# Reordering the start of two MoE layers: table behind the gathers, splits behind the activations, transposes on TensorE

## The chip, the cores and the metric

The kernel runs on one core of a Trainium2 chip. The metric is device time in microseconds of one execution, the median of the runs. The engines are TensorE (PE in the profile, its weight loads PEld), VectorE (DVE), ScalarE (ACT), GpSimd (POOL) and SyncE (SP), which here only issues DMAs; each runs its own instructions in order and waits on semaphores for the others.

## What is computed

Sparse attention over 4 batches, 8 heads, 576 positions and head size 64 (four heads with a window of 32, four with every fourth of 128 positions), then two mixture-of-experts layers with one expert for each of 2304 tokens.

```python
def reference(...):
    attn = softmax(where(mask, q @ k.T / 8, -1e9)) @ v      # 4 x 8 x 576 x 64
    x = attn.transpose(0, 2, 1, 3).reshape(2304, 512)
    # first MoE, 8 experts, w1 512 x 1024, w2 1024 x 512
    e = argmax(x @ w_gate)
    x = softmax(x @ w_gate)[e] * sigmoid(x @ w_output_gate)[e] * (relu(x @ w1[e]) @ w2[e])
    # second MoE, same shapes
    l = x @ w_gate2 + modality_bias[modality_id]
    e = argmax(l)
    return softmax(l)[e] * (relu(x @ w1b[e]) @ w2b[e])
```

Every float32 factor of a product is held as a high and a low float16 part ("hi" and "lo"), and three of the four products are summed. So each expert's weights, 4 MB in float32, are loaded to `raw`, and split: the high part on ScalarE (L100), the low part on VectorE (L105) or GpSimd.

## The kernel before

**The attention** runs over 16 head pairs in an order written out by hand (`ORDER`, `iteration`), and ends in `tail` (L556), where the last two pairs are finished while the weights of the first expert are split: `his` splits high parts on ScalarE, `los` low parts on VectorE. A piece is 1024 columns of `raw`; there are eight, four of w1 and four of w2. Before the tail, in iteration 14, `lo_in_place` (L111) makes the low part of piece 0 with two GpSimd instructions (L113, L114). `stM` (L394) builds the softmax mask of a pair from six tiny operations, on VectorE for the last pair; `stMT` transposes it on TensorE and copies it on ScalarE (L425). `stH` (L467) and `stZ` (L474) split a pair's result; `stZ` runs on GpSimd except for the last pair. `fs()` steps `first_slots`, which finds the first 256 tokens of the commonest expert and gathers their rows.

**Each MoE** (`moe`, L885) works through slots of 128 tokens. `slot` (L956) multiplies with w1 in two halves of 48 products (`mm1`), applies relu and splits each half (`hsplit`: high on ScalarE L943, low on VectorE L944), and multiplies with w2 in 24 products (L1006): for each of eight chunks the high part with w2's high and low part, then the low part with w2's high part. Slots 0, 1 and 2 use the first expert; slot 3 (`KE`) is the first with weights that the sorted table chooses. Around a slot's products lie numbered hooks; `at(s, k, ...)` puts work at hook k of slot s, in the order in which the engines get it. Hook 1 lies inside the first half of the w1 products, hook 2 after it, 3 after the first `hsplit`, 5 after the second, 9 and 6 after 4 and 12 of the 24 products, 7 after the last.

**The sort** (`sort`, L708) is a generator whose steps are placed at hooks. It computes each token's expert and rank; `ob` and `obp` (one-hot of the block, L811, L812); `table()` (L776), some twenty VectorE operations that decide which expert each slot has; the rank matrix `A` (L820); with `A` and `obp` on TensorE the index of each slot's tokens (L825); gathers of three slots' rows on GpSimd (L896); then the gates, and at the end two sums over `A` (L871, L873). In the first MoE `first` is true: `obp` is made on GpSimd, and `table()` with the eight weight loads of slot 3 (`start.weights`) comes ahead of `A`. In the second MoE they come after the gathers.

`first_splits(FIRST[i])` splits two pieces of slot 3's weights and loads the two after them for slot 4. `x_turned` (L907) brings the gathered rows of a slot into column form by eight TensorE transposes and a ScalarE copy; `x_transpose` (L899) does it by a DMA transpose. `post1.out` (L1132) scales a slot's result and splits it into a row; `post1.transposes` (L1143) stores the row and, for results 0 and 1 (`TURN` is 2), turns it by a DMA transpose; `post1.turn` (L1152) turns later ones on TensorE; `post1.router` multiplies with the second router's weights.

## Time and profile before

| what | us |
|---|---|
| median of 3 runs | 660.13 (657.55 to 660.41) |
| profiled execution, its own time | 657.82 |
| its span, first to last instruction | 656.0 |
| TensorE busy | 595.0 (91% of the span) |
| VectorE busy | 364.8 (56%) |
| ScalarE busy | 271.0 (41%) |
| GpSimd busy | 206.6 (31%) |
| mean granted clock of TensorE | 0.967 |

The attention takes the first 155 us, the first MoE runs to about 436 us, the second from there. In the profile an idle stretch of an engine is put down to the instruction that released it ("PE plg L1168 <- DMA yT" says that TensorE waited at line 1168 for the DMA that wrote `yT`). The granted clock is a share of 2.4 GHz; 0.50 is 1.2 GHz. Times in a timeline are microseconds from the span's start: start, duration, engine, line, operation, output and inputs, count.

### The profile page before, as it was taken

The numbers are of one execution on the slowest core, as the hardware profiler recorded it, in microseconds if no ns is written. First come the engines' busy times: TensorE is split into PE (matmuls) and PEld (weight loads), VectorE is DVE, ScalarE is ACT, GpSimd is POOL, SyncE is SP. The second block draws the span as 40 slices with busy tenths as digits, with TensorE's granted clock in tenths as the row PEclk, the third lists the DMA queues.
The fourth block names the chain that finished last, engine by engine and source line by source line (L and its number), as shares of the span: only waits on it lengthen the run. The fifth ranks groups of instructions, "written<-read, shape, count | busy, mean of one in ns | idle before, by whom it ended". The sixth has DMA issues, their size and how long they took to land. (4 is left out here: it accounts for less than half of the span.)

```text
span 656.0 us, 19386 instructions
## 1 busy us (share of the span) xinstructions
PE 595.0 (91%) x7393; PEld 461.0 (70%) x7393; DVE 364.8 (56%) x638; ACT 271.0 (41%) x368; POOL 206.6 (31%) x319
## 2 busy tenths in 40 slices
PE   3989798867888999999999999989899999999994
PEld 2878787756656776868677686766576768677772
DVE  6798888888576625963848922249531011113560
ACT  5667676763165124833626611111522112113450
POOL 3657676823282111101010410002542312122220
PEclk9989989986898999999999999999989999999998
DMA  8764849952599973997876862210995424132921
GB/s 281 247 204 160 237 165 314 263 128 69 193 308 263 267 163 86 332 358 159 204 220 203 222 143 67 57 30 23 309 304 124 117 64 98 50 98 84 310 59 40
DMA packets 105088, 115.20 MB, mean 176 GB/s; under 512 B 68623, under 2 KB 73487, under 8 KB 104976
## 3 DMA queue, kind: packets, MB, share of 16 engines
q1 hardware_dynamic: 99296, 95.94, 52.2%
q0 software_dynamic: 5280, 17.13, 8.2%
q8 instruction: 59, 0.97, 0.6%
q10 hardware_dynamic: 400, 0.72, 0.3%
q14 instruction: 53, 0.43, 0.2%
HBM read 209.13 MB, written 18.22 MB: 347 GB/s over the span
## 5 line engine op out<-in xcount | busy, mean ns | idle before, releaser
L933 PEld LDWEIGHTS <-wb 128*128 128x128 f16 x4032 | 233.5, 99 | 10.2 <-DMA xT<-xg 2.6
L933 PE MATMUL ph<-xT,wb 128*128 128x128 f16 x3648 | 214.3, 221 | 3.9 <-DMA xT<-xg 2.6
L944 DVE SCALAR_TENSOR_TENSOR hl<-ph,hh 128x512 f16<-128x512 f32 x84 | 57.7, 689 | 171.5 <-ACTq L952 156.8
L1006 PE MATMUL py<-wb,hh 128*128 128x512 f16 x608 | 137.9, 379 | 0.7 <-ACT hh L943 0.6
L1006 PEld LDWEIGHTS <-hh 128*128 128x128 f16 x672 | 63.6, 98 | 71.6 <-ACT hh L943 3.7
L943 ACT ACTIVATE hh<-ph 128x512 f16<-128x512 f32 x84 | 50.1, 596 | 154.2 <-PE ph L933 147.8
L105 DVE SCALAR_TENSOR_TENSOR wb<-raw,wb 128x1024 f16<-128x1024 f32 (+1 forms) x79 | 103.6, 1350 | 16.2 <-ACT wb L100 13.8
L100 ACT ACTIVATE wb<-raw 128x1024 f16<-128x1024 f32 (+1 forms) x80 | 87.0, 1134 | 7.7 <-ACTq L952 3.0
L1006 PE MATMUL py<-wb,hl 128*128 128x512 f16 x304 | 71.8, 379 | 0.0
L1006 PEld LDWEIGHTS <-hl 128*128 128x128 f16 x336 | 32.9, 98 | 39.6
L1268 POOL DMA_INDIRECT out<-y,idx x16 | 16.1, 1009 | 100.9 <-ACTq L952 84.0
L452 PE MATMUL po<-v,pT 128*96 128x65 f32 x384 | 41.1, 260 | 0.0
L452 PEld LDWEIGHTS po<-v,pT 128*96 128x96 f32 x384 | 38.0, 176 | 0.0
L391 PE MATMUL ps<-kk,qs 128*96 128x128 f16 x192 | 31.1, 235 | 4.1 <-DVE kk L349 2.2
L391 PE MATMUL ps<-kk,ql 128*96 128x128 f16 x192 | 31.3, 236 | 3.5 <-DVE ql L369 3.4
L439 ACT ACTIVATE pT<-pst 128x384 f32<-128x384 f32 x48 | 23.5, 489 | 24.6 <-PE pst L438 23.9
L896 POOL DMA_INDIRECT xg<-x_dram,idxaa x23 | 25.1, 1090 | 26.5 <-DMA xT<-xg 14.3
L392 DVE TENSOR_REDUCE M<-ps 96x4 f32<-96x512 f32 x48 | 31.6, 680 | 3.2 <-PE ps L391 2.8
L391 PEld LDWEIGHTS <-ql 128*96 128x96 f16 x192 | 24.7, 135 | 12.4 <-DVE ql L369 5.1
L436 PE MATMUL pst<-mt,msel 128*128 128x96 bf16 x192 | 30.9, 220 | 2.1 <-ACT mt L425 2.1
L1267 ACT ACTIVATE y<-py,gsb 128x512 f32<-128x512 f32 x16 | 11.0, 686 | 52.4 <-PE py L1006 49.5
L391 PEld LDWEIGHTS <-qs 128*96 128x96 f16 x192 | 25.0, 135 | 8.6 <-issue 4.1
(404 smaller groups left out, 739.0 us busy)
## 6 DMA issues: line engine op xcount, KB each, us to landing
raw<-in_w1a SPq DMA_DIRECT2D x95, 512.0 KB
raw<-in_w2a SPq DMA_DIRECT2D x92, 512.0 KB
raw<-in_w1b SPq DMA_DIRECT2D x75, 512.0 KB
raw<-in_w2b SPq DMA_DIRECT2D x72, 512.0 KB
qk<-in_qk SPq DMA_DIRECT2D x16, 608.0 KB
v<-in_vw SPq DMA_DIRECT2D x16, 390.0 KB
y_dram<-y SPq DMA_DIRECT2D x11, 260.0 KB
y_dram<-lotmp SPq DMA_DIRECT2D x10, 260.0 KB
```

The lines of the kernel that those rows point to most:

```text
L100: nc.scalar.activation(wb[:, 0, s], raw[:, s], AF.Copy, scale=SW)
L105: nc.vector.scalar_tensor_tensor(out=wb[:, 1, s], in0=raw[:, s], scalar=SW, in1=wb[:, 0, s], op0=ALU.mult, op1=ALU.subtract)
L391: nc.tensor.matmul(ps[:, j, :], q[:, h, QT * i:QT * i + QT], kk[:, h, QT * i:QT * i + 128], start=False, stop=w == 1 and j == 3, skip_grou ...
L392: nc.vector.tensor_reduce(out=Ms[n][:, 4 * g:4 * g + 4], in_=ps, axis=AX.X, op=ALU.max)
L436: nc.tensor.matmul(ps[:, j, :], msel[:, typ, j, :], mt[:, g, :], start=j == 0, stop=False, skip_group_check=True)
L439: nc.scalar.activation(pTs[n][:, 4 * g:4 * g + 4, :], ps, AF.Exp, scale=0.125 / (SQK * SQK))
L452: nc.tensor.matmul(po[:, h, i, :], pT[:, NQ * h + i, :], v[:, h, i, :], start=True, stop=True)
L896: nc.gpsimd.indirect_dma_start(t, None, src, bass.IndirectOffsetOnAxis(start.idx[:, s:s + 1], 0))
L933: nc.tensor.matmul(ph[:, j, :], w[:, c, fs], xT[:, parts[c + i], :], start=k == 0, stop=k == 47, skip_group_check=True)
L943: nc.scalar.activation(hs, ph, AF.Relu)
L944: nc.vector.scalar_tensor_tensor(out=hl[:, 4 * g:4 * g + 4, :], in0=ph, scalar=0.0, in1=hs, op0=ALU.max, op1=ALU.subtract)
L1006: nc.tensor.matmul(to, a, w, start=k == 0, stop=k == len(ops) - 1)
```

## The change

- `TURN` becomes 0: no result is turned by a DMA transpose. Results 0 and 1 are turned by TensorE after slot 2 of the first MoE (hook 7), result 1 through the PSUM buffer `pw`, and written out at hooks 5 and 6, behind both activations.
- `lo_in_place` goes; the low parts in `tail` are each one piece earlier, and those of pieces 6 and 7 are made in slot 0. `stZ` runs on VectorE for the last two pairs.
- In the first MoE's sort `obp` is made on VectorE, and `table()` with slot 3's loads comes after the index and the gathers, as in the second MoE. The index is computed within slot 0's second products, at a new hook 10 behind the 20th.
- In slot 0 of the first MoE the second products are in the order high x high, low x high, high x low.
- The splits of slot 3's weights move behind the activations: in the first MoE from hooks (1,3), (1,6), (2,0), (2,1) to (1,5), (1,6), (2,0), (2,3); in the second the first of them from (2,3) to (2,5).
- The rows of slot 3 are turned by TensorE in slot 2 of both MoEs, at hook 1 of the first and hook 2 of the second, instead of by a DMA transpose issued in slot 1.

```diff
@@ -30,7 +30,7 @@
 CA1, CA2, CF = 13, 13, 4
 KA, KE = 2, 3
 NMIN = 18
-TURN = KE - 1
+TURN = 0
 NB = 12
 BIG = 8e12
 SQK = 2.0 ** 5
@@ -107,11 +107,6 @@
         else:
             nc.gpsimd.tensor_scalar(pool[:, 0:n * 512], raw[:, s], SW, None, op0=ALU.mult)
             nc.gpsimd.tensor_tensor(wb[:, 1, s], pool[:, 0:n * 512], wb[:, 0, s], op=ALU.subtract)
-
-    def lo_in_place(wb, k, n=2):
-        s = slice(k * 512, (k + n) * 512)
-        nc.gpsimd.tensor_scalar(raw[:, s], raw[:, s], SW, None, op0=ALU.mult)
-        nc.gpsimd.tensor_tensor(wb[:, 1, s], raw[:, s], wb[:, 0, s], op=ALU.subtract)
 
     def splits(wb, ops, load=None):
 
@@ -471,7 +466,7 @@
             kind = hp // 2
             x16, xh = x16s[b, kind], x_half[b, kind]
             c = slice((hp % 2) * 128, (hp % 2) * 128 + 128)
-            (nc.vector if n == NPR - 1 else nc.gpsimd).tensor_tensor(x16[:, :, 1, c], xh[:, :, c], x16[:, :, 0, c], op=ALU.subtract)
+            (nc.vector if n >= NPR - 2 else nc.gpsimd).tensor_tensor(x16[:, :, 1, c], xh[:, :, c], x16[:, :, 0, c], op=ALU.subtract)
             if hp % 2 == 0:
                 return
 
@@ -556,12 +551,12 @@
         def tail():
             a, b = NPR - 2, NPR - 1
             his(2, 3)
-            los(1)
+            los(0)
             stC(a, 0)
             stH(b - 2)
             stMT(b)
             his(4)
-            los(2, 3)
+            los(1, 2)
             stZ(b - 2)
             stB(b, 0)
             stC(a, 1)
@@ -576,7 +571,7 @@
             his(7)
             stB(b, 2)
             stZ(a)
-            los(4)
+            los(3)
             stC(b, 0)
             fs()
             stX(a, 0)
@@ -589,11 +584,11 @@
             stR(a - 2)
             stR(b - 2)
             stZ(b)
-            los(5)
+            los(4)
             stX(b, 0)
             stX(b, 1)
             stR(a)
-            los(6)
+            los(5)
             fs()
             stR(b)
 
@@ -643,8 +638,6 @@
                     do(f, n + dn, *x)
                 if n == NPR - 2 and o in ('H', 'MT'):
                     his(o == 'MT')
-                if n == NPR - 2 and o == 'P1':
-                    lo_in_place(wbuf[0], 0)
 
         STEP = {'A': (stA, 1), 'B': (stB, 0), 'C': (stC, -1), 'X': (stX, -2), 'K': (khi, 2), 'L': (klo, 2), 'Q': (qsc, 2), 'P': (qsplit, 2)}
         STEP = {k + str(i): v + (i,) for k, v in STEP.items() for i in range(3)}
@@ -705,7 +698,7 @@
             return t
         return T
 
-    def sort(nm, lg, nt, inv, fe, ea, tab, scale, og, extra, gscale, start, first):
+    def sort(nm, lg, nt, inv, fe, ea, tab, scale, og, extra, gscale, start):
 
 
         v, gp, act = nc.vector, nc.gpsimd, nc.scalar
@@ -809,11 +802,8 @@
         sb = [P, nt, NSLOT]
         ob, obp = (T(k, [-1, NSLOT], F16) for k in ("ob", "obp"))
         v.tensor_tensor(ob, bm.unsqueeze(1).to_broadcast(sb), pi[:, 1].unsqueeze(2).to_broadcast(sb), op=ALU.is_equal)
-        (gp if first else v).tensor_tensor(obp, ob, tokv[:, :nt].unsqueeze(2).to_broadcast(sb), op=ALU.mult)
-        yield
-        if first:
-            table()
-            start.weights(KE, always=True)
+        v.tensor_tensor(obp, ob, tokv[:, :nt].unsqueeze(2).to_broadcast(sb), op=ALU.mult)
+        yield
         A = T("A", [-1, P], F16)
         for a in range(0, nt, ACH):
             n = min(ACH, nt - a)
@@ -831,9 +821,8 @@
         start.idx, start.idxf = idx, idxf
         for i in range(KA, KA + 3):
             start.gather(i)
-        if not first:
-            table()
-            start.weights(KE, always=True)
+        table()
+        start.weights(KE, always=True)
         yield
 
         dl = T("dl", [-1, E])
@@ -1001,7 +990,8 @@
             sp(2)
             k = 0
             to = pys[s] if s < KA else py
-            ops = [(a[:, f, :], w[:, f, :]) for a, b_ in ((hh, (w2h, w2l)), (hl, (w2h,))) for f in range(8) for w in b_]
+            order = [(hh, (w2h,)), (hl, (w2h,)), (hh, (w2l,))] if start.late_low and s == 0 else [(hh, (w2h, w2l)), (hl, (w2h,))]
+            ops = [(a[:, f, :], w[:, f, :]) for a, b_ in order for f in range(8) for w in b_]
             for a, w in ops:
                 nc.tensor.matmul(to, a, w, start=k == 0, stop=k == len(ops) - 1)
                 k += 1
@@ -1009,6 +999,8 @@
                     hook(9)
                 if k == 12:
                     hook(6)
+                if k == 20:
+                    hook(10)
             if s >= NMIN - 1:
                 post.router(s - 1)
             elif s >= KE:
@@ -1038,7 +1030,7 @@
         return r
 
     class Start:
-        name, next = "a", NEXT
+        name, next, late_low = "a", NEXT, True
 
         def hook(self, s, k):
             for f in self.plan.get((s, k), ()):
@@ -1149,12 +1141,12 @@
                 return
             self.turn(s)
 
-        def turn(self, s):
+        def turn(self, s, tag="pyt"):
 
             if s is not None and s < TURN:
                 return
             y16 = self.row(s)
-            pt = pp.tile([P, 8, P], F16, name="pyt", tag="pyt")
+            pt = pp.tile([P, 8, P], F16, name=tag, tag=tag)
             for c in range(8):
                 nc.tensor.transpose(pt[:, c, :], y16[:, c * P:(c + 1) * P], identh)
             vt.tensor_copy(self.yT[0 if s is None else s % 2], pt)
@@ -1177,7 +1169,7 @@
                 vt.scalar_tensor_tensor(out=lg2[:, s, :], in0=pl, scalar=1.0 / (SX2 * SWR), in1=lg2[:, s, :], op0=ALU.mult, op1=ALU.add)
 
     post1 = Post1()
-    so1 = sort("a", lg1[:, :, 0:8], NT, None, fe1, early[0], tabs[0], 1 / (SX1 * SWR1), lg1[:, :, 8:16], [midf], SX2 / (SX1 * SW * SW), start1, True)
+    so1 = sort("a", lg1[:, :, 0:8], NT, None, fe1, early[0], tabs[0], 1 / (SX1 * SWR1), lg1[:, :, 8:16], [midf], SX2 / (SX1 * SW * SW), start1)
     fs2 = []
 
     def slots2():
@@ -1197,22 +1189,23 @@
     def at(s, k, *f):
         plan.setdefault((s, k), []).extend(f)
 
-    at(0, 0, run(so1), lambda: lo_piece(wbuf[0], 14))
+    at(0, 0, run(so1), lambda: lo_piece(wbuf[0], 12))
     at(0, 1, run(so1, 2))
     at(0, 2, run(fss))
-    at(0, 5, run(so1))
-    at(1, 0, run(so1, 2))
-    at(1, 3, run(so1), start1.consts, lambda: start1.first_splits(FIRST[0]))
-    at(1, 6, lambda: start1.turned(KA), lambda: start1.transpose(KA + 1), lambda: start1.first_splits(FIRST[1]))
-    at(2, 0, lambda: gt.memset(y16p[1][:, 2 * DM:], 0.0))
-    at(2, 0, lambda: start1.first_splits(FIRST[2]))
-    at(2, 1, lambda: start1.first_splits(FIRST[3]))
+    at(0, 5, run(so1), lambda: lo_piece(wbuf[0], 14))
+    at(0, 10, run(so1, 2))
+    at(1, 3, run(so1), start1.consts)
+    at(1, 5, lambda: start1.first_splits(FIRST[0]))
+    at(1, 6, lambda: start1.turned(KA), lambda: start1.first_splits(FIRST[1]))
+    at(2, 0, lambda: gt.memset(y16p[1][:, 2 * DM:], 0.0), lambda: start1.first_splits(FIRST[2]))
+    at(2, 1, lambda: start1.turned(KA + 1))
     at(2, 2, run(so1))
+    at(2, 3, lambda: start1.first_splits(FIRST[3]))
     for i in range(NSLOT - NMIN):
         at(0, 3, lambda i=i: start1.zero(i))
-    at(2, 3, first_out(post1, start1, 0))
-    at(2, 5, first_out(post1, start1, 1))
-    at(2, 6, lambda: start1.part(KE + 1, *EARLY))
+    at(2, 5, first_out(post1, start1, 0))
+    at(2, 6, first_out(post1, start1, 1))
+    at(2, 7, lambda: post1.turn(0), lambda: post1.turn(1, "pw"), lambda: start1.part(KE + 1, *EARLY))
     at(3, 7, start1.last)
     for s, k in ((3, 5), (3, 7), (4, 3), (4, 5), (4, 7), (5, 5)):
         at(s, k, run(fes2))
@@ -1229,7 +1222,7 @@
     ilast = m1.tile([P, 1], I32, name="ilast")
 
     class Start2(Start):
-        name, next = "b", NEXT2
+        name, next, late_low = "b", NEXT2, False
 
         def fields(self, g, inv, ex):
             self.g = g
@@ -1275,17 +1268,17 @@
             pass
 
     start2, post2 = Start2(), Post2()
-    so2 = sort("b", lg2, NSLOT, start1.inv, fe2, early[1], tabs[1], 1.0, None, [], 1 / (SX2 * SW * SW), start2, False)
+    so2 = sort("b", lg2, NSLOT, start1.inv, fe2, early[1], tabs[1], 1.0, None, [], 1 / (SX2 * SW * SW), start2)
     plan = start2.plan = {}
     at(0, 0, lambda: post1.out(None, py1), lambda: post1.transposes(None))
     at(0, 8, lambda: post1.router(None), run(so2))
     at(0, 5, run(so2))
     at(0, 7, run(so2, 2))
     at(1, 9, run(so2, 2))
-    at(1, 7, lambda: start2.turned(KA), lambda: start2.transpose(KA + 1))
+    at(1, 7, lambda: start2.turned(KA))
+    at(2, 2, lambda: start2.turned(KA + 1))
     at(2, 0, run(so2))
-    at(2, 3, lambda: start2.first_splits(FIRST[0]))
-    at(2, 5, lambda: start2.first_splits(FIRST[1]))
+    at(2, 5, lambda: start2.first_splits(FIRST[0]), lambda: start2.first_splits(FIRST[1]))
     at(2, 6, run(so2), lambda: start2.first_splits(FIRST[2]))
     at(2, 7, lambda: start2.first_splits(FIRST[3]))
     for i in range(KA):
```

`late_low` is true in the first MoE and false in the second.

## Rows read from the trace of the kernel before

**Rows 1.** Waits of TensorE, whole span (waiter, releaser: us in total, times, longest)

```profile
PE pm L423 <- DVE mb L413: 4.1, 1, 4.1
...
PE pidx L825 <- DVE Aa L820: 3.1, 2, 2.2
...
PE ph L933 <- DMA xT<-xg: 2.6, 1, 2.6
...
PE plg L1168 <- DMA yT<-y: 2.4, 1, 2.4
...
PE pya L1006 <- ACT hh L943: 1.5, 1, 1.5
...
PE pg L873 <- POOL lotmp L1207: 1.1, 1, 1.1
```

**Rows 2.** Windows: length, busy PE PEld DVE ACT POOL, clock, DMA share, GB/s

```profile
155.51:216.11 60.60, 51.84 (x586) 39.40 (x586) 42.75 (x90) 24.20 (x31) 24.65 (x41) 0.92 0.74 228
476.23:488.33 12.10, 12.10 (x121) 9.23 (x120) 4.32 (x6) 2.34 (x4) 5.91 (x10) 0.87 0.86 301
488.33:498.87 10.54, 10.54 (x122) 7.71 (x120) 1.38 (x2) 2.57 (x4) 2.56 (x4) 1.00 0.72 183
146.00:148.00 2.00, 1.86 (x36) 1.80 (x35) 1.35 (x4) 0.68 (x1) 0.00 (x0) 0.50 0.00 0
```

**Rows 3.** The timeline of the tail: start, us, engine, line, operation

```profile
129.64 2.12 POOL L114 TENSOR_TENSOR wb<-raw,wb 128x1024 f16<-128x1024 f32 x1
...
129.89 1.91 DVE L410 TENSOR_TENSOR r<-r,mb 96x12 f32<-96x12 f32 x1
...
131.14 0.82 ACT L467 CAST x<-xh 96x768 f16<-96x768 f32 x1
...
133.72 0.16 DVE L413 CAST mb<-r 96x12 bf16<-96x12 f32 x1
...
134.34 0.40 ACT L425 COPY mt<-pm 128x288 bf16<-128x288 bf16 x1 [2.38 <-PE pm L423]
...
141.03 1.47 DVE L241 TENSOR_SCALAR fs_sel<-fs_mi,fe_ma 128x13 f16<-128x13 f32 x1
...
149.91 0.95 DVE L474 TENSOR_TENSOR x<-xh,x 96x768 f16<-96x768 f32 x1
```

**Rows 4.** The timeline of slot 0, and of the second MoE's L812

```profile
158.68 1.20 DVE L105 SCALAR_TENSOR_TENSOR wb<-raw,wb 128x1024 f16<-128x1024 f32 x1
...
164.21 1.28 DVE L944 SCALAR_TENSOR_TENSOR hl<-ph,hh 128x512 f16<-128x512 f32 x2
...
169.13 2.62 DVE L820 TENSOR_TENSOR Aa<-c16t,pia 128x1152 f16<-128x1152 f16 x2
...
169.77 1.98 SPq L92 DMA_DIRECT2D raw<-in_w1a  x4
...
449.24 0.92 DVE L812 TENSOR_TENSOR obpb<-obb,tokv 128x729 f16<-128x729 f16 x1
```

**Rows 5.** The timeline of slot 2 of the second MoE, loads and splits

```profile
459.89 2.42 SPq L92 DMA_DIRECT2D raw<-in_w1b  x4
...
465.83 1.91 ACT L100 ACTIVATE wb<-raw 128x2048 f16<-128x2048 f32 x1 [1.34 <-DMA raw<-in_w1b]
...
474.89 1.91 ACT L100 ACTIVATE wb<-raw 128x2048 f16<-128x2048 f32 x1 [0.73 <-DMA raw<-in_w2b]
```

**Rows 6.** The timeline of slot 1 of the first MoE

```profile
179.95 1.91 ACT L100 ACTIVATE wb<-raw 128x2048 f16<-128x2048 f32 x1
...
183.28 0.61 PE L911 MATMUL pxt<-identh,xg 128*128 128x128 f16 x8
...
183.92 1.01 ACT L912 COPY xT<-pxt 128x1024 f16<-128x1024 f16 x1 [1.58 <-PE pxt L911]
```

**Rows 7.** The timeline of slots 2 and 3 of the first MoE

```profile
202.44 0.53 SPq L1148 DMA_DIRECT2D y_dram<-y  x1
...
206.14 0.69 ACT L1140 ACTIVATE y<-py,gsa 128x512 f16<-128x512 f32 x1 [6.91 <-DMA y_dram<-y]
```

## The prediction

> **What bounds the kernel now.** I read the waits of TensorE over the whole span first. TensorE runs the program in the order written, so what it waits for is what a reordering can win. Apart from the start-up, the list holds six waits where the diff works [rows 1]: for the mask of the last head pair (4.1 us), for the rank matrix `A` (3.1), for slot 3's DMA transpose in the second MoE (2.6), for the DMA transpose of the first result (2.4), for an activation that queues behind a weight split (1.5), and for GpSimd (1.1). Then I read the windows. Slots 0 to 3 of the first MoE last 60.60 us with TensorE busy for 51.84. An undisturbed slot of the second MoE takes 10.54; the one entered after the 2.6 us wait takes 12.10, at a mean granted clock of 0.87 [rows 2]. So such a wait costs its own length and then 1.56 us of matmuls at the lower level. Slots 1 and 3 of the first MoE are entered or crossed in the same way. Between slot 3 and the second MoE the list names no wait, so time won ahead of it should reach the end.
>
> The sum has three parts: the attention's tail (A), slots 0 to 3 of the first MoE (B), slots 2 and 3 of the second (C).
>
> **A, the tail.** The low part of piece 0 leaves GpSimd. Beside it VectorE's tiny mask operations stand still: L410, 96x12, takes 1.91 us while GpSimd runs L114 for 2.12; the cast L413, with GpSimd idle, takes 0.16 [rows 3]. Six such operations at some 0.2 us each give the mask near 130.1 instead of 133.9. Late next is ScalarE: ahead of its copy of the mask it still has L467, to 131.96, so the copy starts near 132.0 instead of 134.34 [rows 3]: 2.35 us. Later L241, 128x13, takes 1.47 us, again beside GpSimd's split of a result; that split goes to VectorE, where its like takes 0.95 [rows 3]. Win 1.3, pay 0.95: 0.35. TensorE's wait shrinks from 4.1 to about 1.9 us, so it may keep its clock there, worth 0 to 1.5 us by the 1.56 above; I take 0.5. The low parts on VectorE in the tail stay six, since the last of them moves into slot 0. Sum: 3.2 us.
>
> Against A speaks that `los(0)` to `los(2)` now run on VectorE just when GpSimd splits the result of pair 13, so the two still meet. By L410's stretch that costs up to 1.7 us [rows 3], by L413's nothing; since the low parts are long and end well before VectorE is wanted next, I take nothing. A: 1.5 to 4.5. The Trainium skill (GPSIMD Engine Reference, Key points) says that GpSimd shares its SBUF interfaces with VectorE and contends with VectorE instructions that have two SBUF inputs, as low parts have. By that rule one of the two would be held for about the other's length, and A would stand near its low end; L410 agrees with its 1.91 us.
>
> **B, slots 0 to 3.** Removed: the waits for `A` 3.1, for the activation 1.5, for GpSimd 1.1, for the DMA transpose 2.4 [rows 1], and twice 1.56 of low clock [rows 2]: 11.2.
>
> Added work of TensorE: eight transposes for slot 3's rows and eight for each of two results, 0.61 a set [rows 6]: 1.8. Three DMA transposes leave SyncE's queue, so the stores and loads behind them go out earlier.
>
> Added waits, place by place:
> - Slot 0. VectorE is the bound. `obp` comes to it from GpSimd: 0.92 for 729 columns in the second MoE [rows 4], so 0.6 for 486. It pushes both low halves, which ended at 165.49, to 166.1, then come `A` (2.62) and a low piece (1.2) [rows 4]. TensorE was free at 168.3 (the first half of `A`, 170.4, less 2.2 of wait [rows 1, 4]), so its 24 second products, half of a slot's 10.54, began near 163.0. In the new order it does eight (1.8), then wants the first low half, ready at 165.5: it stands 0.7. The index product comes at about 168.2, the halves of `A` at 167.4 and 168.7: 0.3. The last low piece is there at 169.9: 0.4. Behind these waits TensorE has only the last four products and slot 1, which starts near 170.4 instead of 172.0. Sum 1.4.
> - Loads of slot 3. The table and the loads it steers move behind `A`, the last low piece and the index on VectorE, and behind three gathers on the DMA queues. The table fills the gap between 165.49 and `A` at 169.13: 3.6 us [rows 4]. Moved, it ends near 173.8, and SyncE issues the eight loads near 174.4 instead of 169.77, 4.6 us later. When do they land? The second MoE has this order already: issue at 459.89, the first pair of pieces split at 465.83, as soon as it is there, the last at 474.89 [rows 5]. That is 5.9 us for the first pair and 3.0 for each further one: 180.3, 183.3, 186.3, 189.3. The first MoE gives a bound from above only: split at 179.95, 10.2 us after issue, with no wait [rows 4, 6]. I take 5.9, since the gathers go ahead there too.
> - Slot 1 to 2. On ScalarE the first split (1.91) now waits for its load; behind it stand the copy of slot 2's turned rows (1.01) and every later activation [rows 6]: 180.3 + 1.9 + 1.0 = 183.2. TensorE is done with slot 1 at 170.4 + 10.54 + 0.6 = 181.6. Wait 1.6.
> - Slot 2. The second activation queues behind the last split, as it queued behind a result's write before; counted on neither side.
> - Slot 3. ScalarE's first act is a write to the row buffer of result 0, whose store must have landed. Before, that was at 206.14, 3.7 us after its issue at 202.44 [rows 7], the issue being held by the DMA transposes. Now the store goes out near the end of slot 2 and lands some 3 us into slot 3. A write, two splits and an activation follow, 3.3 us, against the 6 us until TensorE wants the activation; the second one is late by 0 to 1. I take 0.7.
>
> Sum of added waits 3.7. The longest is like the 1.5 us wait of [rows 1], behind which the clock stayed up, so I add no low clock.
>
> B: 11.2 - 1.8 - 3.7 = 5.7 us. Ends: without the added waits 9.4; with the first pair at the first MoE's 10.2 us, 4.3 later, 1.4.
>
> **C, the second MoE.** Slot 3's rows are turned by TensorE within slot 2: the wait of 2.6 and 1.56 of low clock go [rows 1, 2], 0.6 comes: 3.6 us. Its splits now stand behind the second activation of slot 2; they are paced by loads that take until 474.89 [rows 5], and the two pairs that slot 3 needs first are there by 468.8, so that split in turn (1.91 on ScalarE, 2.4 on VectorE) they are ready near 473.7, when TensorE comes. Late by 1 us, C is 2.6. Range 2.4 to 4.
>
> **Sum.** 3.2 + 5.7 + 3.6 = 12.5 us. The profiled execution took 657.82 us (its span is 656.0), so 645.3. The median of the runs shown, 660.13, is 2.3 above it: 647.6. I write 647.5.
>
> **Rivals.**
> 1. The weights are late. Place: ScalarE in slot 1, where the copy of the turned rows queues behind a split that waits for its load. For it: the loads start 4.6 us later while TensorE comes earlier, and the only bound in the first MoE is 10.2 us. Against it: the 5.9 of [rows 5]. At 10.2 us B is 1.4: 647.5 + 4.3 = 651.8.
> 2. The waits are only renamed: in the tail and the second MoE ScalarE's chain and the loads bound already, so the change does there not what it sets out to. A is 1 and C is 1: 647.5 + 4.8 = 652.3. For it: ScalarE is the next to be late in A by the sum itself. Against it: TensorE's list has no other wait over 1.5 us there.
> 3. Slower, by the lower clock. Place: slots 0 and 1, which TensorE enters from a sparse tail where the granted clock is 0.50, 1.2 GHz [rows 2]. Several short waits have replaced three long ones. If they hold the clock at that level, each microsecond of full-clock matmuls costs another: two slots of 10.54 cost 21 us, 668.5. It decides once more than 12.5 us of such work runs at the low level. Against it: the mean over slots 0 to 3 was 0.92 with longer waits [rows 2].
>
> **How the numbers follow.** Forecast 0.62 (643 to 650.5); late weights 0.18; renamed waits 0.14; low clock 0.06. The range reaches down to B without added waits and with half of what A and C have above my values, 642.5, a little rounded to 642, and up past both middle rivals, with a part of one added to the other, to 655. About 0.5%, 3.3 us, is what a measurement of this kernel can tell from no change. The first two rivals stay faster than that unless they meet in full. So: faster 0.88, within 0.5% 0.06, slower 0.06.
>
> **What would show it.** Right: VectorE's mask chain under 1.5 us and the mask's copy near 132; slots 0 to 3 about 55 us long; slot 3 of the second MoE entered without a DMA wait and as long as the slots after it. Wrong in A: low parts stretched beside GpSimd. Wrong in B: ScalarE's first split of slot 3's weights waiting for its load more than 26 us after slot 0's start, or a new wait of TensorE over 1.6 us. Wrong altogether: a granted clock of 0.5 in slot 1.

## The result, and the profile after

| | before | after |
|---|---|---|
| median, measured side by side (us) | 658.84 (657.00 to 660.41) | 647.68 (647.37 to 648.77) |
| profiled execution, its own time | 657.82 | 648.77 |
| its span | 656.0 | 647.0 |
| TensorE busy | 595.0 | 593.6 |
| mean granted clock | 0.967 | 0.967 |

The ratio is 0.9835, with an interval of 0.9801 to 0.9869: 1.65% faster, about 11 us. The prediction was 647.5. The profiled execution of after is the slowest of its four, so the two traces differ by 9.0 us only. Two later traces of the same kernel (`again`, `again2` below) have spans of 644.3 and 644.9.

The list of TensorE's waits over the whole span comes first again (waiter, releaser: us in total, times, longest). Of the six waits of [rows 1] none is left at its old length:

```profile
PE ph L922 <- ACT xT L901: 2.7, 2, 1.6
PE pst L431 <- ACT mt L420: 2.4, 2, 1.9
...
PE py L996 <- ACT hh L932: 1.7, 2, 1.2
...
PE pyt L1151 <- ACT y L1132: 0.7, 1, 0.7
...
PE pm L418 <- DVE mb L408: 0.3, 1, 0.3
...
PE pidx L815 <- DVE Aa L810: 0.2, 1, 0.2
```

The mask (L418) went from 4.1 to 0.3 us, the index (L815) from 3.1 to 0.2, and the DMA transposes are gone from the list. What is new is ScalarE, in four places: its copy of the mask (1.9), its copy of slot 2's turned rows (1.6 of the first row), slot 3's activation (1.7) and a write of a result (0.7). The windows show where that lies (length, busy PE PEld DVE ACT POOL, clock, DMA share, GB/s): slots 0 to 3 of the first MoE together, then one by one, then slots 2 and 3 of the second MoE. The first answers the first line of [rows 2], and the last, slot 3 of the second MoE, its second line (12.10 us at a clock of 0.87).

```profile
152.29:209.87 57.58, 51.79 (x611) 38.26 (x611) 44.24 (x94) 25.20 (x32) 22.15 (x40) 0.96 0.70 229
...
152.29:167.38 15.09, 14.48 (x150) 10.88 (x150) 13.71 (x36) 2.30 (x4) 2.49 (x13) 0.84 0.05 15
167.38:181.05 13.67, 11.47 (x129) 8.20 (x128) 7.41 (x32) 4.60 (x8) 7.85 (x13) 1.00 0.77 269
181.05:194.58 13.53, 13.38 (x181) 10.43 (x180) 11.62 (x9) 10.58 (x11) 9.11 (x13) 1.00 1.07 342
194.58:209.87 15.29, 12.47 (x154) 8.74 (x154) 11.51 (x21) 7.71 (x10) 2.70 (x4) 1.00 0.94 306
...
456.15:468.87 12.72, 12.72 (x182) 9.88 (x182) 6.39 (x7) 7.28 (x8) 7.16 (x10) 1.00 1.12 344
468.87:479.41 10.54, 10.54 (x121) 7.71 (x120) 6.79 (x7) 4.51 (x5) 8.82 (x13) 1.00 0.95 343
```

Slot 0 starts at 152.29 instead of 155.51: 3.2 us (part A). Slots 0 to 3 last 57.58 instead of 60.60: 3.0 us (part B). Slots 2 and 3 of the second MoE last 23.26 (456.15 to 479.41) instead of 27.38 (460.95 to 488.33): 4.1 us (part C). Where slot 2 of the second MoE began before is read from TensorE's timeline of the kernel before; slot 4 began where the third line of [rows 2] does.

```profile
460.95 5.52 PE L933 MATMUL ph<-xT,wb 128*128 128x128 f16 x96 [1.12 <-ACT xT L912]
```

The sum of the three parts is 10.4. Of it 1.4 is lost again on the way: 0.7 between slot 4 and the second MoE, and 0.7 in the second MoE's slots 0 and 1, whose first 96 products took 5.74 + 1.06 us instead of 5.07 + 0.61. In `again` these products took 5.07 + 0.61 as before, in `again2` 5.70 + 1.06, behind the same wait of 1.68 us. The granted clock over this stretch is 0.81 in the first trace (430.93 to 438.00) and 1.00 in `again` (429.30 to 435.50). So the low level came in two of three traces of one kernel; it is one reason why these traces differ by up to 2.7 us.

**The tail.** The timeline (start, us, engine, line, operation, output and inputs, count, in brackets the wait and its releaser), to be held against [rows 3]:

```profile
130.00 0.16 DVE L408 CAST mb<-r 96x12 bf16<-96x12 f32 x1
130.09 4.95 DVE L105 SCALAR_TENSOR_TENSOR wb<-raw,wb 128x1024 f16<-128x1024 f32 x3
...
131.95 0.39 ACT L420 COPY mt<-pm 128x288 bf16<-128x288 bf16 x1
132.12 1.82 POOL L469 TENSOR_TENSOR x<-xh,x 96x768 f16<-96x768 f32 x1 [5.21 <-ACT x L462]
132.39 0.20 PE L431 MATMUL pst<-mt,msel 128*128 128x96 bf16 x1 [1.87 <-ACT mt L420]
...
138.09 0.24 DVE L236 TENSOR_SCALAR fs_sel<-fs_mi,fe_ma 128x13 f16<-128x13 f32 x1
...
139.61 1.21 DVE L105 SCALAR_TENSOR_TENSOR wb<-raw,wb 128x1024 f16<-128x1024 f32 x1
```

The tiny operations take 0.16 or 0.17 us each, the mask ends at 130.2, and ScalarE copies it at 131.95: these are the 130.1 and 132.0 of the prediction. The contention that the prediction weighed is there too: three low parts take 4.95 us while GpSimd runs L469, where one alone takes 1.21. That is 1.3 us more. No loss from it can be seen: the product that VectorE works on next ended on TensorE at 134.68, the low parts at 135.04, and TensorE has no wait between 132.39 and 138.38. L236 fell from 1.47 to 0.24.

**Slots 1 to 3.** The timeline of SyncE's loads and stores and of ScalarE, to be held against [rows 4, 6, 7]:

```profile
171.48 1.78 SPq L92 DMA_DIRECT2D raw<-in_w1a  x4
...
178.19 1.91 ACT L100 ACTIVATE wb<-raw 128x2048 f16<-128x2048 f32 x1 [3.12 <-DMA raw<-in_w1a]
...
180.01 0.99 ACT L901 COPY xT<-pxt 128x1024 f16<-128x1024 f16 x1
...
181.05 1.95 PE L922 MATMUL ph<-xT,wb 128*128 128x128 f16 x32 [1.65 <-ACT xT L901]
...
191.72 1.08 SPq L92 DMA_DIRECT2D raw<-in_w2a  x2
192.91 0.43 SPq L1140 DMA_DIRECT2D y_dram<-y  x1
...
200.33 0.69 ACT L1132 ACTIVATE y<-py,gsa 128x512 f16<-128x512 f32 x1 [8.04 <-DMA y_dram<-y]
```

Two transfers set the pace in this trace. The first pair of slot 3's weights is issued at 171.48 and split at 178.19, 6.7 us later, with ScalarE waiting for it. The copy of slot 2's rows stands behind that split, and TensorE waits 1.65 us for the copy. And the store of row 0 is issued at 192.91, right behind two loads; ScalarE wants to write into the same buffer and gets it at 200.33, 7.4 us later. Before, it was 3.7 us [rows 7]. What that does to TensorE in slot 3 is this:

```profile
201.08 0.40 PE L1151 MATMUL pyt<-identh,y 128*128 128x128 f16 x4 [0.68 <-ACT y L1132]
201.86 0.40 PE L1151 MATMUL pyt<-identh,y 128*128 128x128 f16 x4 [0.39 <-DVE y L1133]
203.45 1.90 PE L996 MATMUL py<-wb,hh 128*128 128x512 f16 x8 [1.20 <-ACT hh L932]
205.83 1.90 PE L996 MATMUL py<-wb,hh 128*128 128x512 f16 x8 [0.48 <-ACT hh L932]
```

Four waits, 2.75 us together, all behind ScalarE's late write.

### The profile page after: what moved, and what is told of

Read it like the earlier page. It is cut to its first block, busy times and chain, and to the rows that moved or that the text cites. A ratio compares the mean times of both kernels' runs of the same rounds, so it can differ in the third digit from the quotient of the medians.

```text
span 647.0 us, 19443 instructions
## 1 busy us (share of the span) xinstructions
PE 593.6 (92%) x7425; PEld 459.1 (71%) x7425; DVE 363.9 (56%) x643; ACT 273.0 (42%) x370; POOL 198.2 (31%) x315
## 5 line engine op out<-in xcount | busy, mean ns | idle before, releaser
L922 PEld LDWEIGHTS <-wb 128*128 128x128 f16 x4032 | 230.7, 99 | 10.1 <-issue 5.1
L922 PE MATMUL ph<-xT,wb 128*128 128x128 f16 x3648 | 211.1, 219 | 3.2 <-ACT xT L901 2.7
L105 DVE SCALAR_TENSOR_TENSOR wb<-raw,wb 128x1024 f16<-128x1024 f32 (+1 forms) x80 | 104.9, 1350 | 16.5 <-ACT wb L100 14.3
L433 PE MATMUL pst<-ql,kk 128*128 128x96 f16 x192 | 30.6, 219 | 0.0
```

Of the source, the lines that this page charges most:

```text
L105: nc.vector.scalar_tensor_tensor(out=wb[:, 1, s], in0=raw[:, s], scalar=SW, in1=wb[:, 0, s], op0=ALU.mult, op1=ALU.subtract)
L433: nc.tensor.matmul(ps[:, j, :], kk[:, h, QT * i:QT * i + 128], q[:, h, QT * i:QT * i + QT], start=False, stop=w == 1 and j == 3, skip_grou ...
L922: nc.tensor.matmul(ph[:, j, :], w[:, c, fs], xT[:, parts[c + i], :], start=k == 0, stop=k == 47, skip_group_check=True)
```

## The experiments

The changed kernel was timed again beside the experiments on other chips, as `again` (the chip of `u_tail`, `u_second` and `u_turn`, where before took 656.35 us) and as `again2` (the chip of `s_load`, `f_both_2` and `u_gz`, where before took 659.46). `u_table`, `f_row`, `f_copy` and `f_both` ran later on the chip of `again`, beside a before of 658.16.

| kernel | median us | range | ratio to before, with interval |
|---|---|---|---|
| again | 646.72 | 646.03 to 648.02 | 0.9855 (0.9802 to 0.9908) |
| u_tail | 649.69 | 649.11 to 650.45 | 0.9891 (0.9838 to 0.9944) |
| u_second | 651.86 | 649.36 to 652.70 | 0.9926 (0.9893 to 0.9959) |
| u_turn | 647.78 | 645.91 to 649.80 | 0.9855 (0.9801 to 0.9910) |
| u_table | 654.48 | 652.22 to 655.77 | 0.9925 (0.9895 to 0.9956) |
| f_row | 645.03 | 644.66 to 645.69 | 0.9791 (0.9742 to 0.9839) |
| f_copy | 647.01 | 644.19 to 648.09 | 0.9827 (0.9778 to 0.9876) |
| f_both | 644.65 | 643.85 to 645.00 | 0.9782 (0.9733 to 0.9830) |
| again2 | 646.57 | 646.28 to 646.72 | 0.9809 (0.9785 to 0.9832) |
| s_load | 645.30 | 644.20 to 645.85 | 0.9788 (0.9762 to 0.9815) |
| f_both_2 | 644.98 | 644.47 to 645.85 | 0.9786 (0.9760 to 0.9812) |
| u_gz | 648.02 | 645.08 to 649.33 | 0.9828 (0.9789 to 0.9867) |

**The changed kernel again.**

> The changed kernel itself, as the base for the kernels beside it. If its three gains are real and not one execution's luck, slot 0 of the first MoE starts near 152.3 us (before: 155.5), slot 4 near 209.9 (216.1), the second MoE's slot 4 near 479.4 (488.3), and the time is 647.7 within 1 us. If the profiled execution was an odd one, these landmarks move by more than 1 us.

> The changed kernel itself, beside the others on the same chip, as the point that they are compared with: 646 to 648.

Its parts in these traces: A 3.7 and 3.2, B 2.9 and 4.0, C 4.1 in both. The predicted 5.7 for B is outside all three. How long the first MoE's slots last (us) shows that B falls short in different places; `f_row` and `s_load`, which change one thing each, come below.

| | slot 0 | slot 1 | slot 2 | slot 3 | sum |
|---|---|---|---|---|---|
| before | 16.53 | 14.27 | 13.98 | 15.82 | 60.60 |
| after | 15.09 | 13.67 | 13.53 | 15.29 | 57.58 |
| again | 15.16 | 13.90 | 15.53 | 13.09 | 57.68 |
| again2 | 15.07 | 13.52 | 13.99 | 14.04 | 56.62 |
| f_row | 15.19 | 13.84 | 13.67 | 11.91 | 54.61 |
| s_load | 15.03 | 13.60 | 15.12 | 11.61 | 55.36 |

In `again` the store of row 0 costs little: TensorE stands 0.9 us in slot 3, not 2.75. There the loss lies at the entry of slot 2. TensorE's timeline and the window of slot 2 in `again`:

```profile
180.83 2.40 PE L922 MATMUL ph<-xT,wb 128*128 128x128 f16 x32 [2.75 <-ACT xT L901]
```

```profile
180.83:196.36 15.53, 15.00 (x180) 12.05 (x180) 12.02 (x10) 10.93 (x11) 6.96 (x11) 0.89 1.04 339
```

The wait for the copy of slot 2's rows is 2.75 us here against 1.65, and the products behind it run at a mean clock of 0.89, which makes slot 2 some 1.6 us longer up to the end of its w1 products.

**One part of the change undone at a time.** First the tail:

```diff
-            los(0)
+            los(1)
...
+                if n == NPR - 2 and o == 'P1':
+                    lo_in_place(wbuf[0], 0)
...
-            (nc.vector if n >= NPR - 2 else nc.gpsimd).tensor_tensor(x16[:, :, 1, c], xh[:, :, c], x16[:, :, 0, c], op=ALU.subtract)
+            (nc.vector if n == NPR - 1 else nc.gpsimd).tensor_tensor(x16[:, :, 1, c], xh[:, :, c], x16[:, :, 0, c], op=ALU.subtract)
```

> Only the tail is put back: the low part of piece 0 and the split of pair 14 on GpSimd again, the low parts of the tail one piece later, piece 7 alone in slot 0. If VectorE was held by GpSimd and that cost 3.2 us, slot 0 starts near 155.5 again and the time is 3 us above the changed kernel's, about 650.7, less up to 0.4 because slot 0 has a low part less. If ScalarE's chain was the real bound in the tail, slot 0 starts at most 1 us later and the time is under 649.

The old waits are back: TensorE's wait for the mask is 4.1 us again, as in [rows 1], and the timeline shows both operations of [rows 3] stretched again, to 1.90 us (1.91 there) and 1.65 us (1.47 there).

```profile
129.80 2.12 POOL L114 TENSOR_TENSOR wb<-raw,wb 128x1024 f16<-128x1024 f32 x1
130.05 1.90 DVE L410 TENSOR_TENSOR r<-r,mb 96x12 f32<-96x12 f32 x1
...
141.39 1.65 DVE L241 TENSOR_SCALAR fs_sel<-fs_mi,fe_ma 128x13 f16<-128x13 f32 x1
```

Slot 0 starts at 156.22, 3.9 to 4.5 us later than in the three traces of after, but slot 4 only 2.4 to 3.3 later: slot 0 has one low part less (14.28 us instead of 15.1). The time is 3.0 us above `again`, as forecast, so part A was sized right.

Then the second MoE, with slot 3's rows turned by DMA:

```diff
-    at(1, 7, lambda: start2.turned(KA))
-    at(2, 2, lambda: start2.turned(KA + 1))
+    at(1, 7, lambda: start2.turned(KA), lambda: start2.transpose(KA + 1))
...
-    at(2, 5, lambda: start2.first_splits(FIRST[0]), lambda: start2.first_splits(FIRST[1]))
+    at(2, 3, lambda: start2.first_splits(FIRST[0]))
+    at(2, 5, lambda: start2.first_splits(FIRST[1]))
```

> Only the second MoE is put back: slot 3's rows by a DMA transpose issued in slot 1, its first split ahead of the second activation. If the wait for that transpose and the low clock behind it were the gain, slot 3 is entered with a wait of 2 to 3 us and its first 96 products take 7 instead of 5.5 us: 3.6 to 4.1 us above the changed kernel, about 651.5. If the loads of slot 3's weights pace it anyway, less than 1 us above.

The timeline of TensorE at the entry of slot 3, and the window of that slot:

```profile
470.73 7.14 PE L922 MATMUL ph<-xT,wb 128*128 128x128 f16 x96 [2.16 <-DMA xT<-xg]
```

```profile
470.73:482.88 12.15, 12.15 (x120) 9.30 (x120) 4.29 (x6) 2.43 (x4) 6.38 (x13) 0.86 0.88 315
```

The wait for the DMA transpose costs its 2.16 us and then 1.6 us of products at a clock of 0.86. Slots 2 and 3 last 27.32 us instead of 23.25: the whole 4.1. The time is 5.1 above `again`, 1 more than that. In its trace 0.8 us more is lost at the second MoE's start, at the low level (5.84 + 1.06 us), which `again2` has too; whether that is what the medians differ by is not shown.

The results turned by DMA transposes:

```diff
-TURN = 0
+TURN = 2
```

> Results 0 and 1 are again turned by DMA transposes; all else as changed. By the sum of the prediction this brings back a wait of 2.4 us and 1.6 us of low clock in slot 3 and takes away 1.2 us of transposes on TensorE: 2.8 us slower, about 650.5. If slot 3 is held in the changed kernel by the store of row 0 (which landed 7.4 us after its issue) rather than by anything TensorE does, the two waits lie beside each other: the transposes, which stand ahead of that store, also delay it, and the loss is 3 to 5 us, 651 to 653, with ScalarE's write of result 2 still the last to wait. If the DMA transposes were hidden, less than 1 us.

The timeline of SyncE's queue and of TensorE in slot 3, and then the window of that slot:

```profile
193.92 1.84 SPq L1139 DMA_TRANSPOSE yT<-y  x1
195.85 0.53 SPq L1140 DMA_DIRECT2D y_dram<-y  x1
...
201.29 0.48 PE L1160 MATMUL plg<-wr2h,yT 128*128 128x8 f16 x12 [3.64 <-DMA yT<-y]
```

```profile
194.81:212.66 17.85, 14.21 (x154) 11.18 (x153) 10.72 (x19) 7.46 (x10) 3.57 (x4) 0.81 1.03 296
```

TensorE waits 3.64 us for the transpose and the slot's clock falls to 0.81; slot 4 starts 2.8 to 3.7 us later than in after. In the trace that is what the DMA transpose was said to cost. In time it is not settled: the median is 1.1 above `again`, where 2.8, 3 to 5 or under 1 had been expected, and its runs spread over 4 us, from below those of `again` to above. The profiled one is its slowest, so its trace may show more loss than most runs have.

The table and slot 3's loads ahead of the rank matrix again:

```diff
         yield
+        if first:
+            table()
+            start.weights(KE, always=True)
         A = T("A", [-1, P], F16)
...
-    at(0, 5, run(so1), lambda: lo_piece(wbuf[0], 14))
+    at(0, 5, lambda: lo_piece(wbuf[0], 14), run(so1))
```

> One part put back: the table and slot 3's loads ahead of the rank matrix again, behind the last low part. The loads are issued some 2.5 us earlier and the rank matrix is 3.6 us later. By the sum, TensorE waits for the rank matrix in slot 0 for about 3.9 us instead of 0.4, and perhaps 1.6 us of low clock follow, while the wait at the entry of slot 2 (1.65, for a split that waits for its load) goes: 1.5 to 3.5 us slower. If the late loads were the true price of the order (the rival of late weights), it is as fast as the changed kernel or faster.

It costs 6.8 to 7.9 us against the medians of the changed kernel, far more than expected. Slot by slot: slot 0 lasts 20.25 us instead of 15.09, slot 1 12.24 instead of 13.67, slot 2 19.42 instead of 13.53, slot 3 12.47 instead of 15.29; together 6.8 more. Slot 0 is the matrix: TensorE waits 3.84 and 0.85 us for it and goes on at the low clock (0.50 from 168.8 to 173, 0.89 in slot 1). Slot 1 is the loads: issued early, they no longer hold the first split, as rival 1 has it. The wait at slot 2's entry is gone, and slot 1 is 1.4 shorter in spite of the lower clock. Slot 2 was not expected. The timeline of TensorE, GpSimd and VectorE in this kernel, the wait for the matrix first, then slot 2:

```profile
168.83 0.42 PE L818 MATMUL pidx<-obpa,Aa 128*128 128x27 f16 x9 [3.84 <-DVE Aa L813]
...
183.93 7.01 POOL L859 TENSOR_TENSOR Bga<-oba,g3a 128x486 f16<-128x486 f16 x3
...
184.73 5.35 DVE L105 SCALAR_TENSOR_TENSOR wb<-raw,wb 128x2048 f16<-128x2048 f32 x2 [1.10 <-ACT wb L100]
...
191.95 1.81 PE L866 MATMUL pg<-Bga,Aa 128*128 128x108 f16 x18 [3.95 <-POOL lotmp L1204]
```

The late slot 1 pushed GpSimd's gate products to 183.93, beside VectorE's low parts of slot 3. In the timeline of after the same three run earlier, while VectorE has no low parts:

```profile
177.37 2.92 POOL L855 TENSOR_TENSOR Bga<-oba,g3a 128x486 f16<-128x486 f16 x3
...
180.13 2.30 DVE L105 SCALAR_TENSOR_TENSOR wb<-raw,wb 128x2048 f16<-128x2048 f32 x1 [3.89 <-ACT wb L100]
180.24 3.05 POOL L855 TENSOR_TENSOR Bga<-oba,midf 128x486 f16<-128x486 f16 x1
```

The three take 2.92 us there and 7.01 beside the splits, and TensorE waits 3.95 us for the sums that need them. The fourth, of the same size, shows it the other way round: 3.05 beside a low part in after, 1.00 alone in `u_table`. So the table's place is worth more than the wait for `A`. The trace shows this stretch, but no run tried it by itself, so its share of the time is not shown.

**Pair 14's split back on GpSimd**, the smaller half of part A:

```diff
-            (nc.vector if n >= NPR - 2 else nc.gpsimd).tensor_tensor(x16[:, :, 1, c], xh[:, :, c], x16[:, :, 0, c], op=ALU.subtract)
+            (nc.vector if n == NPR - 1 else nc.gpsimd).tensor_tensor(x16[:, :, 1, c], xh[:, :, c], x16[:, :, 0, c], op=ALU.subtract)
```

> The changed kernel, with the split of pair 14's result on GpSimd as before the change. By the sum of part A: the tiny operation at the first-slot search takes 1.3 us longer again beside GpSimd, the split no longer takes 0.95 of VectorE; slot 0 starts 0.35 us later, time the same within what can be told. Rival (the split on VectorE is itself on TensorE's path, since TensorE waits 0.8 us for it in the changed kernel): slot 0 starts earlier or at the same time.

The timeline of GpSimd and VectorE at that place:

```profile
136.03 1.64 POOL L469 TENSOR_TENSOR x<-xh,x 96x768 f16<-96x768 f32 x1 [3.74 <-ACT x L462]
...
136.42 1.28 DVE L236 TENSOR_SCALAR fs_sel<-fs_mi,fe_ma 128x13 f16<-128x13 f32 x1
```

The tiny L236 is held until GpSimd's split ends (137.70 and 137.67), 1.28 us instead of 0.24. From the mask's last cast to slot 0 there are 22.94 us, against 22.29, 22.72 and 22.85 in the three traces of after: 0.1 to 0.65 more, where 0.35 was predicted. Slot 0 itself starts at 151.28, earlier than in all three (151.77 to 152.32), because the mask's cast ends earlier by more than that; by the sign that was named, a later slot 0, the expectation did not come out. The time, 1.45 above `again2` with overlapping ranges, does not settle a term of this size either.

**What slot 3 waits for.** Row 0 gets a buffer of its own, so that ScalarE's write waits for no store:

```diff
-            return xg2[0] if s == 1 else y16s if s is None else y16p[s % 2]
+            return xg2[1 - s] if s in (0, 1) else y16s if s is None else y16p[s % 2]
```

> One edit on the changed kernel: row 0 is written to a buffer of its own, so that ScalarE's write of result 2 at the head of slot 3 no longer waits for row 0's store. If that wait is what kept the first MoE's gain at 3.0 instead of 5.7 us, TensorE's waits in slot 3 (0.7 and 0.4 for the row, 1.2 and 0.5 for the activations, 2.8 in all) shrink under 0.5, slot 4 starts 2.5 to 2.8 us earlier and the time is 645. If ScalarE is held there by the splits of slot 4's weights and their loads, the label on the wait changes and the time gains less than 0.7 us.

The window of slot 3 and ScalarE's write in it:

```profile
195.41:207.32 11.91, 11.77 (x154) 8.80 (x154) 11.18 (x20) 6.83 (x9) 2.21 (x4) 1.00 0.99 361
```

```profile
194.26 0.69 ACT L1132 ACTIVATE y<-py,gsa 128x512 f16<-128x512 f32 x1 [1.11 <-PE py L996]
```

The write waits for TensorE's product alone, and no wait is left inside the slot: 11.91 us instead of 15.29 (13.1 and 14.0 in the other two traces of after). So the store's landing is what held it. Slots 0 to 3 last 54.61 us, 6.0 less than before, where 5.7 was predicted for B. Slot 4 starts 2.55 us earlier than in after, and the time is 645.03, as expected (645), 1.7 below `again` without overlap. Why the store took 7.4 us is a second question: the next kernel keeps the buffer and issues the four loads that stood ahead of the store behind it.

```diff
-    at(2, 0, lambda: gt.memset(y16p[1][:, 2 * DM:], 0.0), lambda: start1.first_splits(FIRST[2]))
+    at(2, 0, lambda: gt.memset(y16p[1][:, 2 * DM:], 0.0), lambda: start1.first_splits('B8:12'))
...
-    at(2, 3, lambda: start1.first_splits(FIRST[3]))
+    at(2, 3, lambda: start1.first_splits('B12:16'))
...
-    at(2, 6, first_out(post1, start1, 1))
+    at(2, 6, first_out(post1, start1, 1), lambda: start1.first_splits('D8:16'))
```

> The changed kernel, with one thing moved: the last four 512 KB loads of slot 4's weights (the w2 pieces) are issued behind the stores of results 0 and 1 instead of ahead of them. Theory (the row's store waits behind loads that are queued on the same DMA engines): the store of row 0 lands 3.7 to 4.5 us after its issue, as in the kernel before, instead of 6.3 to 7.4; TensorE's waits inside slot 3 fall from 2.0 to 2.8 us to under 1, and slots 0 to 3 last 56 us or less; the loads, issued some 4 us later, are wanted only in the second half of slot 3, so the time is 645 to 646.5, 1 us under the changed kernel on the same chip. Rival (a store of this size takes over 6 us here whatever is queued ahead of it, the 3.7 before being a lucky case): landing 6 us or more, slot 3 as in the changed kernel, time as there. Third case: the store lands soon but the late loads hold the splits of slot 4: slot 4 is entered with a new wait on a load or on ScalarE of 1 us or more, time as the changed kernel or above.

The timeline of SyncE's queue and of ScalarE's write:

```profile
194.08 0.35 SPq L1140 DMA_DIRECT2D y_dram<-y  x1
...
195.20 2.43 SPq L92 DMA_DIRECT2D raw<-in_w2a  x4
...
196.31 0.69 ACT L1132 ACTIVATE y<-py,gsa 128x512 f16<-128x512 f32 x1 [2.83 <-DMA y_dram<-y]
```

Without loads right ahead of it the store lands in 2.2 us. Slot 3 lasts 11.61 us and has no wait inside; a wait of 1.16 us for VectorE stands ahead of it, so that slot 2 is longer. Slots 0 to 3 last 55.36 us together. The late loads hold two splits of slot 4's weights (0.74 and 1.94 us on ScalarE), and TensorE does not notice: slot 4 begins without a wait. The time is 1.3 below `again2`, with no overlap. The store's landing goes by the loads ahead of it: 7.4, 6.3 and 6.2 us with two loads issued 1.2 to 1.7 us before it (three traces of after), 3.7 with four issued 6 to 10 us before it (192.86 to 196.15 in the kernel before, the store at 202.44 [rows 7]), 2.2 here with the last four issued 7 to 12 us before it (182.51 to 187.24, the store at 194.08). A DMA transpose of slot 4's rows also stands ahead of the store, 3.8 us in after and 6.2 in `s_load`. That it alone makes the store late is unlikely, since in before two transposes stood right ahead of the store (issued from 196.25 to 202.35) and it landed in 3.7; no run moved the transpose by itself.

**What slot 2's entry waits for.** The copy of the turned rows goes ahead of the first split:

```diff
-    at(1, 5, lambda: start1.first_splits(FIRST[0]))
-    at(1, 6, lambda: start1.turned(KA), lambda: start1.first_splits(FIRST[1]))
+    at(1, 6, lambda: start1.turned(KA), lambda: start1.first_splits(FIRST[0]), lambda: start1.first_splits(FIRST[1]))
```

> One edit on the changed kernel: in slot 1 ScalarE copies slot 2's turned rows before, not after, the first split of slot 3's weights, which waits for its load. TensorE's wait of 1.65 us at the entry of slot 2 should go and slot 2 start 1.7 us earlier. If slot 3 is held by row 0's store, nearly all of it is given back there: 0 to 0.5 us gained. If the entry of slot 2 was a bound of its own, 1.2 to 1.7 us gained, 646.3.

> Both edits, the buffer of its own for row 0 and the copy ahead of the split. If the store holds slot 3 and the load holds the entry of slot 2, they add up and a little more, since nothing gives the copy's gain back: 3.5 to 4.3 us below the changed kernel, about 643.8. If the splits bind in slot 3, no more than 1.5 us.

> The changed kernel with row 0 in its own buffer and the copy of slot 2's turned rows ahead of the first split, now beside the changed kernel on the same chip. Theory: 2 us under it, 644 to 646, with no wait for the row's store. If the gain seen across chips was the chip's: within 0.7 us of it.

In `f_copy` slot 1 shrinks from 13.67 to 11.81 us and the wait at slot 2's entry is gone, as it should. But slot 2 then lasts 15.71 instead of 13.53, with TensorE idle for 1.8 of it: it waits for activations, which stand behind splits on ScalarE, for GpSimd, and for VectorE's copy at the entry of slot 3. No time can be seen to be won, as one of its two expectations has it; the profiled run is the fastest of five, so its trace shows `f_copy` at its best. Together with row 0's own buffer it brings 0.4 us over `f_row`, less than either spreads: `f_both` is 2.1 us under `again` where 3.5 to 4.3 under the changed kernel was expected. On one chip `f_both_2` is 1.6 us under the changed kernel, without overlap; the timeline of ScalarE in its slot 2 shows that the second and third split still wait for their loads:

```profile
181.20 1.91 ACT L100 ACTIVATE wb<-raw 128x2048 f16<-128x2048 f32 x1 [1.92 <-DMA raw<-in_w1a]
183.83 1.91 ACT L100 ACTIVATE wb<-raw 128x2048 f16<-128x2048 f32 x1 [0.71 <-DMA raw<-in_w2a]
```

So with the store out of the way ScalarE still waits for the loads of slot 3's weights in slot 2. That they are the bound there is argued; no run with row 0's own buffer issued them earlier. `f_both` (644.65 and 644.98) is the fastest version found, 2.1 to 2.2% under the kernel before, though the medians of `f_row` and `s_load` lie within the range of `f_both_2`.

## Why the prediction was right, and where it was not

The time was right to 0.2 us, and that is better than the working deserves. The base was 1.3 us too high (660.13, where before's median side by side was 658.84) and the gain 1.3 too large (12.5, where 11.2 was measured); that the two cancel is luck.

- **A, 3.2 us: right.** Slot 0 came 3.2, 3.7 and 3.2 us earlier in the three traces of after; putting the tail back cost 3.0. Since kernels with this very tail start slot 0 anywhere from 150.71 to 153.45 (eleven traces) and there is one trace of before, these differences alone are good to about 1 us. A closer measure is TensorE's waits of 0.15 us and more from the mask to slot 0: 11.7 us in before, 8.3 in after, 7.7 in `again`. The steps held one by one: the mask near 130.1, the copy at 132.0 behind L462, TensorE's wait 1.87. The low parts did meet GpSimd, for 1.3 us of the 1.7 that stood as the bound, and no loss from it is seen. The reason given for taking nothing was too kind, though: VectorE was wanted 0.3 us before the low parts ended. The Trainium skill (SBUF — State Buffer, section SBUF: two separate sides) describes the pair of ports that VectorE and GpSimd share as an exclusive lock: against a GpSimd instruction that reads SBUF, a VectorE instruction with two SBUF inputs (or in a two-port mode) is blocked until the other is over, or blocks it, by which of them came first. The traces agree: in `u_gz` L236, whose inputs are two tiles, ended at 137.70, GpSimd's L469 at 137.67. So the contention came, and still A did not fall to the low end of its range.
- **C, 3.6 us: right, slightly low.** 4.1 in all three traces, and 4.07 when undone. Its two halves are seen in `u_second`: 2.16 us of wait and 1.6 of low clock. The eight transposes that replace them take 0.61 by themselves but put TensorE's next product only 0.45 later, and slot 3's splits were not late at all.
- **B, 5.7 us: wrong by 1.7 to 2.8.** What was removed was removed: the waits for `A` (0.15 left), for GpSimd and for the DMA transpose are gone, and `u_table` and `u_turn` bring them back. Slot 0 came out at 15.09 for a predicted 14.9. What failed lies behind it, and it is three terms.
  - *Slot 3's store.* It was to land some 3 us into slot 3 and cost TensorE 0.7. In the first trace it landed 5.75 us in, and TensorE stood 2.75; in `again` and `again2` it was 3.6 and 4.5 us in, and 0.9 and 1.7. The 3.7 us from [rows 7] was taken as the store's own duration, although in before that store went out 6 us behind the last loads, and the change itself moved it right behind two. The prediction saw that transposes leave the queue, and not that it had put the store among loads. `s_load` shows it: 2.2 us without them.
  - *The landing of slot 3's first pair.* It took 6.7, 7.1 and 6.6 us instead of 5.9, behind an issue 0.2 to 0.3 later. It makes slot 1 13.5 to 13.9 long where 12.8 was predicted. This term was too small by about 1 us in every trace; why the pair takes longer here than in the second MoE is not shown.
  - *No low clock.* None was added behind the wait at slot 2's entry. In `again` that wait was 2.75 us, and 1.6 more went at the low level behind it; in the other two, at 1.65 and 1.50, the clock stayed at 1.00.

  Against the prediction (14.9, 12.8 and what is left of B, 27.2) slot 0, slot 1 and slots 2 with 3 are 0.2, 0.9 and 1.6 too long in the first trace, which is the 2.7 by which B is short there, and 0.3, 1.1 and 1.4 in `again`. With the store out of the way alone, `f_row`, B is 6.0.
- **The base.** 2.3 us were added because the median shown of before lay that much above its profiled execution. The medians of before in the later comparisons are 656.35, 658.16, 658.84 and 659.46, around the 657.82 of the profile. The term was in the main the noise of a few runs, and it hid part of what B did not bring.
- **The rivals.** Rival 1, late weights, is half there: ScalarE's first split does wait for its load, to 25.9, 26.2 and 25.7 us after slot 0's start in the three traces, around the 26 us that were named as the sign. Slot 2's entry waits 1.65, 2.75 and 1.50 us for a forecast 1.6. That the first trace meets the 1.6 is luck: TensorE itself was 0.9 us late there, with two gaps inside slot 1's products that have no wait in the profile. The 10.2 us of landing did not happen. Rival 2 is refuted by `u_tail` and `u_second`. Rival 3, a low clock throughout, is refuted: the windows have 1.00 in slots 1 to 3, where the mean over slots 0 to 3 had been 0.92 and is 0.96 now. But `again` shows a low clock in one slot (0.89 in slot 2, 0.94 over slots 0 to 3).

## What to carry to other kernels

A duration from issue to landing, as measured here, belonged to what was queued ahead of the transfer more than to the transfer: before a store is moved, list the loads that will be issued ahead of it in the new place, and look at who wants to write into its source buffer. A second buffer or the store ahead of the loads removed that wait here. Where GpSimd and VectorE both have long work, price a reordering also by what will newly run side by side, since here one stood for about the other's length. And read a term from more than one trace of the same kernel before saying where a shortfall lies: B was short by nearly the same amount in two traces, for different reasons.

## What the runs showed of the hardware beyond that

- A row's store of 260 KB landed after 2.2 us (`s_load`), 3.7 (before), and 6.2, 6.3 and 7.4 (the changed kernel), by the loads issued ahead of it on the same queue. `u_tail`, `u_second` and `u_gz`, with the same order as the changed kernel, have 6.1, 6.3 and 7.3. The Trainium skill (DMA: Bandwidth & Descriptors, section Queues, rings and completion order) says that on each DMA engine the descriptors of one ring are consumed in ring order, by which a store queued behind loads starts after them. These numbers fit that; the rings themselves are in no trace here.
- GpSimd's three products of 128x486 took 2.92 us alone and 7.01 beside VectorE's low parts, and VectorE's three low parts 4.95 instead of 3 x 1.21 beside GpSimd. The Trainium skill (GPSIMD Engine Reference, Key points) names a contention of the two for VectorE instructions with two SBUF inputs. The traces agree, since a low part has two, `raw` and `wb`.
- After the same wait of 1.68 us at the start of the second MoE the next 96 products took 5.68 us in one trace of the changed kernel and 6.76 and 6.80 in two others. At the entry of slot 2 of the first MoE a wait of 2.75 us was followed by a clock of 0.89 over the slot in `again`, and waits of 2.77 and 2.79 by 1.00 in `u_second` and `u_turn`. So the length of the wait alone does not settle whether the clock falls.
